# Infini-attention beside a spectral filter on one core: an earlier copy of the products with v, an earlier split for the inverse transform, and maxima that start later

## The chip, the cores and the metric

The kernel runs on one core of one Trainium2 chip. The metric is the device time of one execution in microseconds (us). Three timed runs of the kernel before took 765.5, 766.13 and 767.05 us; the median is 766.13 us. The profile was taken in an execution of its own, which took 768.89 us, of which the recorded span is 767.1 us.

A core has TensorE (PE, matmuls; PEld is its weight load), VectorE (DVE), ScalarE (ACT), GpSimd (POOL) and SyncE (SP). Each works through its own instructions in order. Transfers are issued from the queues of SP and POOL and carried out by 16 DMA engines.

## What is computed

Two independent halves, side by side in the output (2048 rows, 576 columns each):

```python
q,k,v = x@wq, x@wk, x@wv          # 32 heads of width 18, 4 segments of 512 rows
for s in range(4):                # one segment after the other
    p = softmax(q_s k_s^T * scale + mask)       # causal, 512x512 for each head
    a_dot = p @ v_s
    a_mem = phi(q_s) M / (phi(q_s) z + 1e-6)    # memory of the earlier segments
    o_s = g*a_mem + (1-g)*a_dot                 # g = sigmoid(beta), one for a head
    M, z = M + phi(k_s)^T v_s, z + sum(phi(k_s))
a = o @ wo
b = irfft2(rfft2(x) * (w_r + i*w_i))            # 2048 x 576
```

## The kernel before

**Stages.** Four stages follow each other on the core. The forward transform runs first (up to about 103 us of the span). Then come the projections (`projections`, to about 284 us): four segments, in each nine units for q and k (`qk_unit`) and four for v (`v_unit`). Between their matmuls a pace (`Pace`) hands out the vector steps of the transform's middle, among them the last butterflies (`last`, four groups b of ten DVE steps, lines L206 and those around it); `tot` says how many of its steps are spread over the projections, all but 8 of those left. Then the inverse transform (`inverse`, 284 to 373 us) runs together with the first part of the attention (`prologue`), and last the attention loop (`attention`) with its tail.

**Inverse transform.** A loop over u, 16 tiles and two steps to drain. For a tile, `i2` multiplies the split values Y with the table `civ` of that tile (18 matmuls, L296), ACT and DVE evict it as a high and a low part T (L326, L328, L333, L334), and two steps later `i3` multiplies T with `itab` (two halves of 7 matmuls, L307), which is evicted (L312, L314, L315) and stored (`yb`, SP, L316). The split of a tile, `ysplit(u)`, is two ACT copies (high part, L280) and two POOL subtractions (low part, L281); the tiles 0 and 1 are split after the projections, tile u+2 in step u. A table is 384 KB, loaded from POOL's queue (`load_civ`, L266) into one of 3 buffers: three ahead, then u+3 at the end of i2 of tile u.

**Prologue.** In between, the maxima of the scores of the first ten steps are computed (`s1`, three pieces per step: matmuls L624 and L633, reductions on DVE). They need the stacks Qs and Ks, which are gathered on SP's queue in six transfers each (`stack_dmas`, L608, 18 rows of 8 KB, 144 KB each). `inverse` yields 64 times, counted by i from 0; past i=5, three yields of each four go to the prologue (`if i>5 and i%4!=3`). With each piece of `s1` a queue of transfers is worked off, two in each three pieces. Four small transfers write the value -1 into two rows of each Ks buffer (L558, POOL's queue).

**Attention loop.** t counts 133 steps; k=t//4 is a block of four heads, n a group of two blocks. In step t: `s1(t+10)` (maxima for a block that comes later), `s2(t)` (scores once more, exponentials on ACT, L668, L673, L677; after the fourth head of a block four selections of the causal triangle, on POOL for k<29, L680, on DVE after, L681), `pv` for the block before (L696, PSUM tile `pvt`, one buffer), and 1.2 steps of a background queue. `pv` of block k is finished in a step with t%4==3; `pv_out` (L702, ACT) copies it to U in the step after that, and `u_dmas` stores U. A new block's pv begins in the next step with t%4==1 and needs the PSUM buffer back. The background queue holds, for each segment, the memory term (`mem1`, L765 to L772), the combination with it (`combine`: L794, L799, then on POOL the sum `am`, L800, and the low part `ol`, L790, with the high part `oh` on ACT, L789) and the output projection (`oproj`, L815). The stacks of group n+2 and n+3 are queued at the first step of group n.

**Tail.** After the loop the last segment's U goes to memory and returns as `ux` in another layout; `last_tile` scales and combines it (L825, L826), `last_proj` multiplies it with wo (L844).

Of the kernel before, what the change touches and what calls it, by code (L numbers as in the profile page):

```python
# [5 lines left out]
F32=mybir.dt.float32; F32R=mybir.dt.float32r  # L6
# [96 lines left out]
class FFT:  # L103
# [152 lines left out]
    def inv_setup(s,cp):  # L256
        nc,io=s.nc,s.io
        s.cp=cp; s.civ={}
        s.itab=cp.tile([128,2,2,2,FP],F32R,name="itab",bufs=1); s.itab2=cp.tile([128,2,FP],F32R,name="itab2",bufs=1)
        nc.gpsimd.dma_start(s.itab,io["itab"].rearrange("p (h r c f) -> p h r c f",h=2,r=2,c=2))  # L260
        nc.gpsimd.dma_start(s.itab2,io["itab2"].rearrange("p (r f) -> p r f",r=2))
        for u in range(3): s.load_civ(u)
    def load_civ(s,u):
        b,a=divmod(u,4)
        cc=s.cp.tile([128,2,384],F32R,name="civ",bufs=3)
        s.nc.gpsimd.dma_start(cc,s.io["civ"][4*a+b].rearrange("p (h m) -> p h m",h=2))  # L266
        s.civ[u]=cc
    def last(s):

        for b in range(4):  # L270
            x=[s.Z[:,b,c] for c in range(4)]
            yield from s.bf(x,x,True)
            s.done=b
    def ysplit(s,u):
        nc=s.nc; b,a=divmod(u,4); x=s.Z[:,b,a]
        while s.done<b and s.pace.one(): pass
        Y=[s.yp.tile([128,2,356],F32R,name=f"Y{i}",bufs=3) for i in range(2)]
        def parts(y): return y[:,:,:256],y[:,:,256:355].rearrange("p q (k c) -> p q k c",k=3)
        X=x[:,:,:256],x[:,:,None,256:289].to_broadcast([128,2,3,33])
        for z,y in zip(X,parts(Y[0])): nc.scalar.copy(y,z)  # L280
        for z,h,l in zip(X,parts(Y[0]),parts(Y[1])): nc.gpsimd.tensor_tensor(l,z,h.bitcast(F32),op=OP.subtract)  # L281
        s.Yt[u]=Y
    def inverse(s,yl,pp):

# [1 line left out]
        T={}; po={}; Yt=s.Yt  # L286
        def i2(u,cs):
            Y=Yt[u]; cc=s.civ[u]
            p=pp.tile([128,len(cs),256],F32,name="i2",tag="i2")
            for k,c in enumerate(cs):  # L290
                n=0
                for (i,hl) in ((0,0),(0,1),(1,0)):
                    for q in range(2):
                        o=128 if q==0 else 0
                        m=128 if c<2 else 99
                        nc.tensor.matmul(p[:m,k],Y[i][:,q,c*128:c*128+m],cc[:,hl,o:o+256],start=n==0,stop=n==5)  # L296
                        n+=1
            return p
# [21 lines left out]
        for u in range(18):  # L320
            if u>15: flush()
            if u<16:
                h=yl.tile([128,3,256],F32R,name="T0",bufs=3); l=yl.tile([128,2,256],F32R,name="T1",bufs=3)
                T[u]=(h,l)
                p=i2(u,(0,1))
                nc.scalar.copy(h[:,:2],p)  # L326
                if u+2<16: s.ysplit(u+2)
                v.tensor_tensor(l,p,h[:,:2].bitcast(F32),op=OP.subtract)  # L328
                yield
                flush()  # L330
                p=i2(u,(2,))
                Yt.pop(u); s.civ.pop(u)
                nc.scalar.copy(h[:99,2],p[:99,0])  # L333
                v.tensor_tensor(h[64:97,2],p[64:97,0],h[64:97,2].bitcast(F32),op=OP.subtract)  # L334
                if u+3<16: s.load_civ(u+3)
                yield
            if u>1:
                yield from i3(u-2)
                out(u-2)
                s.pace.take(1)  # L340
# [36 lines left out]
class ATT:  # L377
# [147 lines left out]
    def projections(s,xp,tp,pp,wv,pace,hook):  # L525
# [4 lines left out]
        def advance():  # L530
            for l in list(live):
                try: next(l)
                except StopIteration: live.remove(l)
        tot=pace.left-8
        for g in range(4):
            if g<3: xq=[s.xprep(g+1,t,(xp,s.x0)[g%2],xp,[128,512],"xst",2) for t in range(5)]
            for i in range(13):
# [16 lines left out]
    def att_setup(s,cp):  # L554
        nc,io=s.nc,s.io
        s.Qs=[cp.tile([128,8,512],BF,name=f"Qs{i}") for i in range(3)]
        s.Ks=[cp.tile([128,8,512],BF,name=f"Ks{i}") for i in range(4)]
        for i in range(4): nc.gpsimd.dma_start(s.Ks[i][108:110].rearrange("p h c -> p (h c)"),io["neg1"])  # L558
        s.mask=cp.tile([128,512],F32,name="mask"); nc.sync.dma_start(s.mask,io["mask"]); s.tri=cp.tile([128,128],BF,name="tri"); s.idb=cp.tile([128,128],BF,name="idb")
        s.bt,s.gt,s.g1=[cp.tile([128,1],F32,name=n) for n in ("bt","gt","g1")]  # L560
        nc.sync.dma_start(s.bt,io["beta"])
        d=lambda n,sh,dt: s.dp.tile(sh,dt,name=n)
        s.uD=[d(f"uD{i}",[576,512],F32) for i in range(4)]
        s.rD=[d(f"rD{i}",[32,512],F32) for i in range(4)]
        nc.sync.dma_start(s.rD[3][24:32],io["neg1"][0:1].rearrange("o (h c) -> (o h) c",c=512))
        s.dD=[None]+[d(f"dD{i}",[32,512],F32) for i in range(1,4)]
        s.rrD=[d(f"rrD{i}",[96,512],BF) for i in range(4)]
        s.rdD=[None]+[d(f"rdD{i}",[96,512],BF) for i in range(1,4)]
# [210 lines left out]
    def combine(s,g):  # L779

        nc=s.nc; tp=s.tp; xs=s.ux
        s.oh=[None]*5; s.ol=[None]*5
        yield
        yield
        for t in range(7):
            if t>1:
                u=t-2; r=126 if u<4 else 72; x=s.am[u]
                s.oh[u]=tp.tile([126,512],F32R,name="oh",bufs=5); s.ol[u]=tp.tile([126,512],F32R,name="ol",bufs=5)
                nc.scalar.copy(s.oh[u][:r],x[:r])  # L789
                nc.gpsimd.tensor_tensor(s.ol[u][:r],x[:r],s.oh[u][:r].bitcast(F32),op=OP.subtract)  # L790
            if t<5:
                r=126 if t<4 else 72; x=xs[t]
                pb=s.ps.tile([126,512],F32,name="pb",tag="post")
# [3 lines left out]
                    nc.vector.tensor_tensor(s.am[t][:r],x[:r],pb[:r],op=OP.mult)  # L797
                else:
                    nc.vector.tensor_tensor(x[:r],x[:r],pb[:r],op=OP.mult)  # L799
                    nc.gpsimd.tensor_tensor(s.am[t][:r],x[:r],s.am[t][:r],op=OP.add)  # L800
                if t<2: s.later(1,lambda t=t: s.ux_load(g,t+3))
            yield
    def oproj(s,g):
# [53 lines left out]
    def prologue(s):  # L857

        nc,io=s.nc,s.io
        for f in s.stack_dmas(0,0)+s.stack_dmas(0,1): f()  # L860
        yield
        s.load_v(0)
        q=s.stack_dmas(1,0)+s.stack_dmas(1,1)+s.stack_dmas(2,1)+[lambda: s.load_v(1)]
        for i in range(2): yield
        s.masks()
        i=0
        for t in range(10):
            for _ in s.s1(t):
                if q and i%3<2: q.pop(0)()
                i+=1  # L870
                yield
            if t in (3,7): m=s.mpath(t//4); next(m)
            if t in (4,8): next(m); next(m,None)
        assert not q
# [3 lines left out]
    def attention(s,tp,ps):  # L878
# [20 lines left out]
        for t in range(133):  # L899
# [1 line left out]
            if t==3: nc.gpsimd.memset(s.cap,3.0e38)  # L901
            if t==4: nc.gpsimd.affine_select(out=s.cap,in_=s.cap,pattern=[[1,128]],compare_op=OP.is_ge,fill=0.0,base=0,channel_multiplier=-1)
            if hh==0 and qd==0:
                if n+2<16: q+=s.stack_dmas(n+2,0)
                if n+3<16: q+=s.stack_dmas(n+3,1)
                if n+2<16: q.append(lambda n=n: s.load_v(n+2))
            st=t%32
            if 16<=t<21: s.pq_load(1,t-16)
# [26 lines left out]
            steps(b,1)  # L935
            if hh==3 and m is not None: steps(m,1)
            if hh==1 and k+2<32: m=s.mpath(k+2); next(m)
            if t>=8 and t%4==0:
                s.pv_out((t-8)//4)
                if t%8==4:  # L940
                    u=s.u_dmas((t-12)//8)
                    if t<124: s.later(1,lambda u=u: qu.extend(u))
                    else: qu+=u
            for l in list(lane):
# [72 lines left out]
def emit(nc,tc,io):  # L1017
    def pool(es,name,bufs=1,**kw):
        return es.enter_context(tc.tile_pool(name=name,bufs=bufs,reuse_waits="tile",**kw))
    with ExitStack() as L0:  # L1020
# [9 lines left out]
        with tc.manual_schedule():  # L1030
# [5 lines left out]
            with ExitStack() as es:  # L1036
# [3 lines left out]
                def hook(g,i):  # L1040
                    if g==3 and i==9:
# [2 lines left out]
                        F.yp=pool(Ri,"yp",2); F.Yt={}; ci=pool(Ri,"ci")  # L1044
                        tc.swap_default_side()
                        F.inv_setup(ci)
                A.projections(xp,tp,pp,wv,F.pace,hook)
                F.ysplit(0); F.ysplit(1)
            Rv.close(); L1x.close()
            with ExitStack() as L1:  # L1050
                cp2=pool(L1,"cp2"); sm=pool(L1,"sm",2); sp=pool(L1,"sp",3)
# [2 lines left out]
                with ExitStack() as es:  # L1054
# [3 lines left out]
                    A.psm,A.mtag=pi,"mt"  # L1058
                    pr=A.prologue(); next(pr)
                    for i,_ in enumerate(F.inverse(yl,pi)):  # L1060
                        if i>5 and i%4!=3: next(pr,None)
                    for _ in pr: pass
                Ri.close(); Rz.close()
                with ExitStack() as es:
# [20 lines left out]
```

## Time and profile before

| | |
|---|---|
| median of three timed runs | 766.13 us |
| the profiled execution | 768.89 us |
| its span | 767.1 us |
| PE busy | 709.8 us, 93% |
| DVE busy | 549.3 us, 72% |
| ACT busy | 461.5 us, 60% |
| POOL busy | 214.6 us, 28% |
| DMA | 121.06 MB, mean 158 GB/s |

Matmuls overlap in PE's pipeline, and a busy PE is not always one at its peak: the clock that was granted to it stands beside (PEclk, 1.00 is full speed). A row of the timeline has start, duration, engine, line, operation, output and inputs, shapes, and in square brackets the idle time before it with what ended it. A row of the chain has start, duration and what the end of the program hung on. A row of the waits has: engine, line, whom it waited for, then us in total, times, and the longest. A row of the windows has the stretch, its length, the busy time of PE, PEld, DVE, ACT and POOL with the count of instructions, then PEclk, the share of the DMA engines, and GB/s.

### The profile page before, as it was taken

The numbers are of one execution on the slowest core, as the hardware profiler recorded it, in microseconds if no ns is written. First come the engines' busy times: TensorE is split into PE (matmuls) and PEld (weight loads), VectorE is DVE, ScalarE is ACT, GpSimd is POOL, SyncE is SP. The second block draws the span as 40 slices with busy tenths as digits, with TensorE's granted clock in tenths as the row PEclk, the third lists the DMA queues.
The fourth block names the chain that finished last, engine by engine and source line by source line (L and its number), as shares of the span: only waits on it lengthen the run. The fifth ranks groups of instructions, "written<-read, shape, count | busy, mean of one in ns | idle before, by whom it ended". The sixth has DMA issues, their size and how long they took to land.

```text
span 767.1 us, 14531 instructions
## 1 busy us (share of the span) xinstructions
PE 709.8 (93%) x5007; PEld 506.5 (66%) x5007; DVE 549.3 (72%) x1278; ACT 461.5 (60%) x1012; POOL 214.6 (28%) x411
## 2 busy tenths in 40 slices
PE   5998999999999996999988999989999899997897
PEld 5987779789798786999644444434665346652387
DVE  6999878997888883686777778776557575664333
ACT  3666794774783733344577777775556565666421
POOL 2110000101101035355254334452235723347010
PEclk9999999999999997899999999999999899998999
DMA  9874535553642388676477656766355564331141
GB/s 334 284 242 122 165 131 182 199 168 120 210 175 97 146 274 189 157 205 181 132 173 175 173 139 157 178 169 148 100 152 147 138 154 118 99 93 39 26 156 65
DMA packets 83245, 121.06 MB, mean 158 GB/s; under 512 B 11352, under 2 KB 50630, under 8 KB 83036
## 3 DMA queue, kind: packets, MB, share of 16 engines
q1 hardware_dynamic: 76580, 104.11, 47.4%
q0 software_dynamic: 6592, 16.03, 7.4%
q8 instruction: 39, 0.64, 0.4%
q14 instruction: 34, 0.28, 0.1%
HBM read 81.78 MB, written 38.24 MB: 156 GB/s over the span
## 4 chain that ended last, share of the span: by engine, by line
PE 64%; DMA 11%; ACT 4%; DVE 3%; issue 2%; POOL 2%; SPq 1%; ACTq 0%; DVEq 0%; POOLq 0%
PE pj L451 11%; PE pv L696 8%; PE pjv L451 7%; PE s L624 7%; PE po L815 6%; DMA Ks<-qkD 5%; PE i L307 4%; PE i L296 3%; DMA ux<-uD 2%; PE s L667 2%; PE pn L765 2%; PE po L844 2%; PE s L671 2%; PE pm L508 2%; DMA Qs<-qkD 1%
## 5 line engine op out<-in xcount | busy, mean ns | idle before, releaser
L628 DVE CUSTOM_DVE_ANT_0 junk<-s,mask 128x512 bf16<-128x512 f32 (+1 forms) x256 | 141.1, 551 | 67.1 <-PE s L624 63.6
L624 PE MATMUL s<-Ks,Qs 108*128 108x384 bf16 (+3 forms) x512 | 139.7, 304 | 10.2 <-DMA Ks<-qkD 3.0
L634 DVE TENSOR_REDUCE mx<-s 128x4 f32<-128x512 f32 x128 | 87.9, 687 | 19.8 <-PE s L633 18.0
L696 PE MATMUL pv<-P,vs 128*32 128x512 f32 (+3 forms) x1024 | 91.6, 452 | 10.3 <-ACT U L702 9.1
L680 POOL TENSOR_SCALAR_AFFINE_SELECT P<-P 128x512 f32<-128x512 f32 x116 | 70.1, 634 | 74.6 <-ACT P L668 65.1
L624 PEld LDWEIGHTS <-Qs 108*128 108x128 bf16 x512 | 50.8, 99 | 60.3 <-issue 42.4
L668 ACT ACTIVATE P<-s 128x512 f32<-128x512 f32 x128 | 77.3, 604 | 21.8 <-PE s L667 18.2
L677 ACT ACTIVATE P<-s 128x256 f32<-128x256 f32 x128 | 49.4, 386 | 54.6 <-PE s L676 54.3
L673 ACT ACTIVATE P<-s 128x512 f32<-128x512 f32 x128 | 77.0, 602 | 0.7 <-PE s L672 0.5
L451 PE MATMUL pj<-xh,wqkl 128*128 128x512 f32 x180 | 71.1, 395 | 0.0
L451 PE MATMUL pj<-xh,wqkh 128*128 128x512 f32 x180 | 71.0, 395 | 0.0
L451 PE MATMUL pj<-xl,wqkh 128*128 128x512 f32 x144 | 61.8, 429 | 0.0
L667 PE MATMUL s<-Qs,Ks 110*128 110x512 bf16 x128 | 49.1, 384 | 1.9 <-DMA Qs<-mts 1.3
L206 DVE TENSOR_TENSOR Z<-t,t 128x290 f32<-128x290 f32 (+1 forms) x96 | 48.6, 553 | 0.1
L296 PE MATMUL i<-civ,Y 128*128 128x256 f32 (+1 forms) x288 | 43.2, 305 | 5.5 <-DMA civ<-civ 3.0
L451 PE MATMUL pjv<-wvh,xh 128*128 128x288 f32 x160 | 48.1, 303 | 0.0
L451 PE MATMUL pjv<-wvl,xh 128*128 128x288 f32 x160 | 46.2, 295 | 0.0
L206 DVE TENSOR_TENSOR t<-Z 128x580 f32<-128x580 f32 x64 | 45.6, 754 | 0.0
L696 PEld LDWEIGHTS pv<-P,vs 128*32 128x32 f32 x1024 | 23.0, 109 | 32.8 <-issue 21.4
L296 PEld LDWEIGHTS i<-civ,Y 128*128 128x128 f32 (+1 forms) x288 | 39.8, 199 | 7.2 <-issue 3.2
L498 POOL MEMSET vt<- 128x32 f32 x16 | 2.3, 161 | 150.7 <-PE pm L508 129.0
L633 PE MATMUL s<-tri,idb 128*128 128x128 bf16 x256 | 43.4, 221 | 0.0
(166 smaller groups left out, 1652.9 us busy)
## 6 DMA issues: line engine op xcount, KB each, us to landing
qkD<-sp SPq DMA_DIRECT2D x36, 384.0 KB
Qs<-qkD SPq DMA_DIRECT2D x96, 144.0 KB
Ks<-qkD SPq DMA_DIRECT2D x96, 144.0 KB
xin<-xb SPq DMA_DIRECT2D x16, 384.0 KB
cfw<-cfw POOLq DMA_DIRECT2D x16, 384.0 KB, 4.3
civ<-civ POOLq DMA_DIRECT2D x16, 384.0 KB, 5.0
vs<-vD SPq DMA_DIRECT2D x16, 330.0 KB
vD<-vt SPq DMA_DIRECT2D x16, 311.0 KB
```

The lines of the kernel that those rows point to most:

```text
L206: v.tensor_tensor(o,a,b,op=op)
L296: nc.tensor.matmul(p[:m,k],Y[i][:,q,c*128:c*128+m],cc[:,hl,o:o+256],start=n==0,stop=n==5)
L451: s.nc.tensor.matmul(out,a,b,start=i==0,stop=i==len(L)-1)
L624: nc.tensor.matmul(out,Q[:108,h,128*i:128*i+128],K[:108,h,:128*(i+1)],start=True,stop=True)
L628: nc.vector.tensor_tensor_reduce(out=junk[:,:w],in0=src,in1=s.mask[:,512-w:],scale=1.0,scalar=-3.0e38, op0=OP.add,op1=OP.max,accum_out=s.m ...
L634: nc.vector.tensor_reduce(out=s.mx[k][:,hh],in_=pa.rearrange("p (b c) -> p b c",c=128),axis=mybir.AxisListType.X,op=OP.max)
L667: nc.tensor.matmul(p0,kk(0),q(0),start=True,stop=True)
L668: nc.scalar.activation(P[0][:,hh],p0,AF.Exp,scale=SC)
L673: nc.scalar.activation(P[1][:,hh],p1,AF.Exp,scale=SC)
L677: nc.scalar.activation(P[2][:,hh],p2,AF.Exp,scale=SC)
L680: if k<29: nc.gpsimd.affine_select(out=x,in_=x,pattern=pat+[[1,128]],compare_op=OP.is_ge,fill=0.0,base=0,channel_multiplier=-1)
L696: nc.tensor.matmul(s.pvt[32*hh:32*hh+32,128*j:],vt[:,j,19*h:19*h+32],mv[0][:,hh,mv[1]],start=j==0,stop=j==2,skip_group_check=True)
```

## The change

- Split of tiles 0 and 1: issued in the last two v units of the last segment, with the low part on DVE in place of POOL. Tiles 2 to 15 as before.
- `civ`: four buffers, four tables loaded ahead, then table u+4.
- `i2` of tile 1 uses the two PSUM buffers of `i3`.
- The pace leaves 10 steps of the butterflies for the inverse, in place of 8.
- The prologue gets yields past i=11 of `inverse` in place of i=5. Its queue of transfers holds two more stacks (Qs of group 2, Ks of group 3) and is worked off one entry a piece, with one more at pieces 0 and 24. The loop does not load these two stacks any more. The transfers of -1 are issued after the steps 2 to 5 of the prologue.
- `pv_out` and `u_dmas` one step earlier: in the step in which pv is finished.
- `combine`: `am` and `ol` on DVE from step 118 on (`s.now` is the step before).

```diff
-        for u in range(3): s.load_civ(u)
+        for u in range(4): s.load_civ(u)
...
-    def ysplit(s,u):
-        nc=s.nc; b,a=divmod(u,4); x=s.Z[:,b,a]
+    def ysplit(s,u,eng=None):
+        nc=s.nc; eng=eng or nc.gpsimd; b,a=divmod(u,4); x=s.Z[:,b,a]
...
-        for z,h,l in zip(X,parts(Y[0]),parts(Y[1])): nc.gpsimd.tensor_tensor(l,z,h.bitcast(F32),op=OP.subtract)
+        for z,h,l in zip(X,parts(Y[0]),parts(Y[1])): eng.tensor_tensor(l,z,h.bitcast(F32),op=OP.subtract)
...
-            p=pp.tile([128,len(cs),256],F32,name="i2",tag="i2")
+            p=pp.tile([128,len(cs),256],F32,name="i2",tag="i3" if u==1 else "i2")
...
-                if u+3<16: s.load_civ(u+3)
+                if u+4<16: s.load_civ(u+4)
...
-        tot=pace.left-8
+        tot=pace.left-10
...
-        for i in range(4): nc.gpsimd.dma_start(s.Ks[i][108:110].rearrange("p h c -> p (h c)"),io["neg1"])
...
+        eng=lambda: nc.vector if s.now>=117 else nc.gpsimd
...
-                nc.gpsimd.tensor_tensor(s.ol[u][:r],x[:r],s.oh[u][:r].bitcast(F32),op=OP.subtract)
+                eng().tensor_tensor(s.ol[u][:r],x[:r],s.oh[u][:r].bitcast(F32),op=OP.subtract)
...
-                    nc.gpsimd.tensor_tensor(s.am[t][:r],x[:r],s.am[t][:r],op=OP.add)
+                    eng().tensor_tensor(s.am[t][:r],x[:r],s.am[t][:r],op=OP.add)
...
-        q=s.stack_dmas(1,0)+s.stack_dmas(1,1)+s.stack_dmas(2,1)+[lambda: s.load_v(1)]
+        q=s.stack_dmas(1,0)+s.stack_dmas(1,1)+s.stack_dmas(2,0)+s.stack_dmas(2,1)+[lambda: s.load_v(1)]+s.stack_dmas(3,1)
...
-                if q and i%3<2: q.pop(0)()
+                for _ in range(1+(i%24==0)):
+                    if q: q.pop(0)()
...
+            if 2<=t<6: nc.gpsimd.dma_start(s.Ks[t-2][108:110].rearrange("p h c -> p (h c)"),io["neg1"])
...
-                if n+2<16: q+=s.stack_dmas(n+2,0)
-                if n+3<16: q+=s.stack_dmas(n+3,1)
+                if 0<n<14: q+=s.stack_dmas(n+2,0)
+                if 0<n<13: q+=s.stack_dmas(n+3,1)
...
-            if t>=8 and t%4==0:
-                s.pv_out((t-8)//4)
-                if t%8==4:
-                    u=s.u_dmas((t-12)//8)
+            if t>=7 and t%4==3:
+                s.pv_out((t-7)//4)
+                if t%8==3:
+                    u=s.u_dmas((t-11)//8)
...
+                    if g==3 and i>10: F.ysplit(i-11,nc.vector)
                 A.projections(xp,tp,pp,wv,F.pace,hook)
-                F.ysplit(0); F.ysplit(1)
...
-                        if i>5 and i%4!=3: next(pr,None)
+                        if i>11 and i%4!=3: next(pr,None)
```

More of the change, by code (lines that the diff above doesn't have):

```diff
@@ L261, in inv_setup @@
         nc.gpsimd.dma_start(s.itab2,io["itab2"].rearrange("p (r f) -> p r f",r=2))
-        for u in range(3): s.load_civ(u)
+        for u in range(4): s.load_civ(u)
     def load_civ(s,u):
         b,a=divmod(u,4)
-        cc=s.cp.tile([128,2,384],F32R,name="civ",bufs=3)
+        cc=s.cp.tile([128,2,384],F32R,name="civ",bufs=4)
         s.nc.gpsimd.dma_start(cc,s.io["civ"][4*a+b].rearrange("p (h m) -> p h m",h=2))
```

## The prediction

> **What bounds the kernel now.** I read the page first, then the chain of waits, then PE's waits, and then windows and timelines of the places where PE stands idle.
>
> ```profile
> PE 709.8 (93%) x5007; PEld 506.5 (66%) x5007; DVE 549.3 (72%) x1278; ACT 461.5 (60%) x1012; POOL 214.6 (28%) x411
> 274.26 9.30 PE pjv L451 x70
> 291.80 13.62 DMA Ks<-qkD
> 305.42 2.00 issue
> 322.33 1.42 PE i L296 x12
> 327.10 1.42 PE i L296 x12
> 360.43 2.15 PE i L296 x18
> 362.58 1.88 PE i L307 x14
> 372.70 0.34 PE L624 MATMUL s<-Ks,Qs 108*128 108x384 bf16 x1
> ```
>
> PE is busy for 93% of the span, so time can come only from its idle places and from a reduced clock. In the chain the projections' last matmuls end at 274.26+9.30=283.56, the inverse stage ends at 372.70, where the loop's first matmul starts, and between them the chain is not PE's work but a transfer of Ks until 305.42 and 2.00 us more. What would the stage cost with PE never waiting? A tile is 2.15 (i2) plus 1.88 (i3), 4.03 us; tiles that carry three pieces of maxima follow each other at 327.10−322.33=4.77 us, so three pieces cost 0.74. Sixteen tiles and thirty pieces are 16×4.03+10×0.74=71.9 us. The stage takes 372.70−283.56=89.1. Some 17.2 us of it are idle time and half clock, nearly all before 314 us:
>
> ```profile
> 284.56 1.01 PE L296 MATMUL i<-civ,Y 128*128 128x256 f32 x4 [1.01 <-ACT Y L280]
> 286.22 7.49 PE L296 MATMUL i<-civ,Y 128*128 128x256 f32 x32 [0.65 <-POOL Y L281]
> 294.42 2.42 PE L296 MATMUL i<-civ,Y 128*128 128x256 f32 x18 [0.70 <-DVE T L328]
> 301.69 3.04 PE L296 MATMUL i<-civ,Y 128*128 128x256 f32 x18 [2.98 <-DMA civ<-civ]
> 307.43 0.48 PE L624 MATMUL s<-Ks,Qs 108*128 108x384 bf16 x1 [2.70 <-issue]
> 284.00:289.00 5.00, 3.71 (x15) 3.02 (x16) 1.08 (x3) 1.98 (x5) 3.86 (x5) 0.70 0.63 169
> ```
>
> PE waits for the split of tile 0, for its low part, for an eviction before tile 2, for the fourth table, and for Ks; and between 284 and 289 its clock averages 0.70. The attention loop has its own places:
>
> ```profile
> PE pv L696 <- ACT U L702: 9.1, 17, 3.4
> PE s L624 <- DMA Ks<-qkD: 3.0, 3, 1.8
> 384.00:388.00 4.00, 2.25 (x19) 0.87 (x18) 1.88 (x8) 1.81 (x6) 0.76 (x3) 1.00 0.82 192
> 692.32 1.27 POOL L800 TENSOR_TENSOR am<-ux,am 126x512 f32<-126x512 f32 x1
> 692.64 0.63 ACT L789 CAST oh<-am 126x512 fp32r<-126x512 f32 x1
> 695.21 3.62 POOL L800 TENSOR_TENSOR am<-ux,am 126x512 f32<-126x512 f32 x1
> 695.22 2.49 DVE L681 TENSOR_TENSOR P<-P,cap 128x512 f32<-128x512 f32 x4
> 698.86 0.62 ACT L789 CAST oh<-am 126x512 fp32r<-126x512 f32 x1 [2.44 <-POOL am L800]
> 700.28 1.94 PE L696 MATMUL pv<-P,vs 128*32 128x512 f32 x8 [3.43 <-ACT U L702]
> 700.00:705.00 5.00, 4.71 (x14) 1.31 (x14) 0.00 (x0) 2.51 (x6) 4.31 (x5) 0.50 0.02 2
> 711.86 1.06 PE L696 MATMUL pv<-P,vs 128*32 128x512 f32 x8 [0.38 <-ACT U L702]
> 722.07 1.14 PE L696 MATMUL pv<-P,vs 128*32 128x512 f32 x8 [1.21 <-ACT U L702]
> ```
>
> One sum on POOL takes 3.62 us beside DVE's minima, where another took 1.27; ACT stands behind it for 2.44, and with it the copy of U and PE for 3.43; then PE runs at half clock for 5 us.
>
> **The change part by part.**
>
> *Start of the inverse.* With tiles 0 and 1 split during the last v units, PE goes from 283.56 straight into tile 0. The two splits leave the place behind the projections:
>
> ```profile
> 283.88 1.92 ACT L280 CAST Y<-Z 128x512 fp32r<-128x512 f32 x4
> 284.98 3.62 POOL L281 TENSOR_TENSOR Y<-Z,Y 128x512 fp32r<-128x512 f32 x4 [2.47 <-ACT Y L280]
> L328 DVE TENSOR_TENSOR T<-i,T 128x512 fp32r<-128x512 f32 x16 | 11.1, 691 | 21.1 <-ACT T L326 21.1
> 270.00:280.00 10.00, 10.00 (x76) 9.88 (x76) 10.00 (x19) 3.08 (x7) 1.30 (x6) 1.00 1.03 349
> 288.50 6.37 SPq L608 DMA_DIRECT2D Ks<-qkD  x6
> ```
>
> ACT's 1.92 us move to where ACT is busy for 3.08 of 10, and cost nothing. DVE is full there; a subtraction of 512 columns takes 0.69 (L328), with the short one I estimate 1.1 us a tile, 2.2 in all, less two steps that the pace gives up. DVE then ends a microsecond later, in time for the first T, which is needed two tiles on; if it were not, the price is that microsecond. The third and fourth PSUM buffer move the wait for an eviction (0.70) back by one tile. The fourth table, loaded ahead, removes the 2.98.
>
> But all this only brings PE sooner to the next thing that is late, and that is Ks. Its transfers are issued by SP behind the last vt store, at 288.50 as before, and landed at 305.42; PE's first maximum ran at 307.43. I assume the same for the changed kernel. The first piece then stands behind i2 of tiles 0 to 4, i3 of 0 and 1 and half of i3 of tile 2, where it stood behind i2 of 0 to 3 and i3 of 0. PE waits all the same, but has done one i2 and one and a half i3 more: 2.15+1.5×1.88=**5.0 us**. Bounds: if tables 4 to 6, now asked for some 4 us sooner, push Ks back by the time of one 384 KB table at 194 GB/s (2.0 us; between the 169 of 284 to 289 and the 219 of 320 to 330, quoted below), 3.0; if Ks comes before PE does, up to the 17.2. I stay by the lower one, since nothing in the change issues Ks sooner.
>
> *Later in the inverse.* A tile moves one table (384 KB), one output (290) and three stacks (432) in place of two: 1106 KB in 4.77 us, 232 GB/s.
>
> ```profile
> 320.00:330.00 10.00, 10.00 (x82) 9.44 (x80) 8.95 (x22) 4.68 (x13) 4.57 (x6) 1.00 0.76 219
> L608 SPq DMA_DIRECT2D Ks<-qkD x6: 265/305/1914, 288.5 to 293.0; - x6
> 299.75 0.37 SPq L316 DMA_DIRECT2D yb<-yout  x1
> ```
>
> 219 GB/s took 0.76 of the DMA engines, so 232 fit at about 0.8: no cost. Past i=11 the prologue gets 39 of the yields and needs 32, so its pieces still end beside tile 14. The four transfers of -1 leave POOL's queue at the start (cover: POOL waits there anyway) and come back between the tables: nothing.
>
> *Start of the loop.* Twelve stack transfers less in the first steps. The gap around 386 (2.25 us busy of 4) is the 1.8 us wait for Ks, and half of the other 1.2 goes with it: **2.4 us**; bounds 0 and 3.0.
>
> *The copy of U.* One step sooner it stands in ACT's queue behind the exponential of a matmul that PE runs after pv, so ACT can't wait in it, and PE's next pv finds its buffer free. 9.1 us of waits: 5.0 of them are the three late ones above (3.43, 0.38, 1.21), the other 4.1 in 14 places. I take half of these, since DVE and ACT are close behind PE: **2.0** (0 to 4.1). Of the 0.38 and 1.21 I take **1.2** (0 to 1.6).
>
> *Combination on DVE.* From step 118 sum and low part take 0.69 on DVE. The 3.62 us sum goes. What is late next: DVE has six such instructions (two low parts, two products, two sums, 4.1 us) before its minima. They can begin when the high part of 692.64 is there, at 693.3, so the minima start by my estimate at 697.4 rather than 695.22; the first is done at 698.1, and pv can start at 698.2 in place of 700.28: 2.1. The idle time falls from 3.43 to about 1.3, and if the clock stays up, half of the 4.71 us at 0.50 returns: 2.4. Together **4.5** (2.1 to 5.8).
>
> The Trainium skill, "TensorE: Matmul & The Clock Gate", section "Part 1: The HAM clock gate", says that the clock is halved after an idle window of about 3.4 us. The 3.43 before 700.28 agrees; the stretch from 284 to 289, halved after gaps of 1.01 and 0.65, does not. By the rule 1.3 us of idle time are harmless and the sum stands; by that row they may cost the clock again, and the sum is 2.4 smaller. The row at 384 to 388, with 1.75 idle at 1.00, decides for the first.
>
> *Tail.*
>
> ```profile
> 727.85 0.86 PE L696 MATMUL pv<-P,vs 128*32 128x128 f32 x16
> 731.24 0.59 ACT L702 COPY U<-pv 128x512 f32<-128x512 f32 x1
> 737.86 0.38 PE L824 MATMUL pb<-rr,sel 96*126 96x512 bf16 x1 [1.69 <-DVE ux L825]
> ```
>
> The last pv ends at 728.71 and U is copied at 731.24, 2.5 us later, behind the output projection's copies. One step sooner it starts the chain U, rD, ux that long before, which covers the 1.69 us for which PE waits in it: **1.7** (0 to 1.7). PE's work behind stays.
>
> Sum: 5.0+2.4+2.0+1.2+4.5+1.7=16.8 us. Against the profiled execution's 768.89 that is 752.1; that execution is 2.8 above the median of the runs, and from the median 766.13 it is **749.3 us**.
>
> **The rivals.** *Ks comes in time.* If the Ks transfers, without the fourth table and the -1 rows beside them, land by about 301, PE barely waits, and the stage gives halfway between 5.0 and 17.2, 11: 743.3. For it: the queue moved only 169 GB/s around their start. Against: tables 4 to 6 take the place. Chance 0.22.
>
> *The transfers take it back.* Tables asked for sooner delay Ks and each other. A table took 9.1 us to land at the median in this stretch (below), tile 4 needs its table 2×2.15+2×4.03=12.4 us after the start, and it can be asked for only when tile 0 is through and POOL has split tile 2, by my estimate 5.5 us in: 2.2 us late, and 2.0 for Ks. The stage then gives 0.8; if the waits for U don't pay either (2.0 and 1.2), 749.3+4.2+3.2=756.7. Chance 0.20.
>
> ```profile
> DMA to landing us min/median/max: 5.7/9.1/10.9
> ```
>
> *SP's queue becomes the bound.* One Ks issue took 1.91 us, where the median of the six is 0.31. With three stacks and an output store (0.37) a tile, SP's time passes the tile's 4.77 once a stack issue takes over 1.47 us. At 1.91 a tile takes 6.1, ten tiles 13.3 us more, and the start's 5.0 and the loop's 2.4 are lost too: 749.3+13.3+7.4=770.0, slower. Against: single event, in a stretch where twelve stacks were issued back to back. Chance 0.04. The Trainium skill, "DMA: Bandwidth & Descriptors", section "Why a DMA increments its semaphore by 16 and not by 1", says that a transfer is spread over the largest number of engines up to 16 that divides its outer sizes; for 18 rows that is 9 by my reading, and it speaks against three stacks a tile. No view here shows the engines apart.
>
> *Nothing changes*, because DVE and ACT take over as the bound wherever PE stops waiting: within 0.2% of 766.13. Chance 0.04; the idle gaps above are too long for it.
>
> **How the numbers follow.** The forecast, 749.3, has 0.50. Its own bounds put it between 745 and 754. The range goes from 741, below the first rival, to 758, above the second; outside lie the last two rivals (0.08) and the far end of the first. A measurement of this kernel can tell about 0.2% (1.5 us) from no change: faster 0.92, same 0.04, slower 0.04.
>
> **What would show it.** Right: L296 starts by 283.7 at clock 1.00 with no wait for Y; no wait for a table at tile 3; the first L624 at 305 to 307.5, behind 2.5 times L307 x14; the loop's first L667 near 368; no wait for Ks in the loop's first 20 us; L800 at 0.69 on DVE and no PE gap over 1.5 us around its end; waits of pv for U under 3 us in all; no gap before the first L824. Wrong: a first L624 later than 309, waits for `civ` above 3 us, PE at half clock after the combination, or SP's stack issues above 1.5 us.

## The result, and the profile after

The kernel after took 747.5 us, median of six runs (746.4 to 749.99), where the kernel before took 765.85 in the six runs beside it (762.87 to 767.05): a ratio of 0.9771, 95% interval 0.9747 to 0.9795. The profiled execution took 747.36 us, of which the span is 745.5; PE's mean clock over the span rose from 0.976 to 0.988. The forecast was 749.3 us, in a range of 741 to 758. Ratios in this document leave out two executions that stand apart as slow, one of the kernel before (773.58 us) and one of e10_sooner (1692.82 us, its other five 751.43 to 759.45).

The page of the kernel after, two lines of it (its lines of code from the attention on stand one lower than before: L623 was L624, L695 was L696, L701 was L702):

```profile
PE 700.2 (94%) x5007; PEld 502.8 (67%) x5007; DVE 553.9 (74%) x1288; ACT 458.7 (62%) x1012; POOL 203.1 (27%) x401
L695 PE MATMUL pv<-P,vs 128*32 128x512 f32 (+3 forms) x1024 | 89.5, 444 | 0.1
```

The second line is the group of all pv matmuls; behind its last bar stands PE's idle time before them, now 0.1 us. The waits for U are gone. PE's own work is the same 5007 matmuls: of the 21.6 us that the span lost, 9.6 are busy time, with the clock higher, and 12.0 are idle time.

The start of the inverse, PE's timeline of the kernel after, and below it the chain of waits there:

```profile
283.88 5.12 PE L296 MATMUL i<-civ,Y 128*128 128x256 f32 x41
289.23 1.82 PE L296 MATMUL i<-civ,Y 128*128 128x256 f32 x13 [0.23 <-POOL Y L281]
298.94 1.11 PE L307 MATMUL i<-itab,T 128*128 128x290 f32 x7
310.08 0.48 PE L623 MATMUL s<-Ks,Qs 108*128 108x384 bf16 x1 [10.03 <-DMA Ks<-qkD]
```
```profile
289.08 7.22 DMA Qs<-qkD
296.32 13.46 DMA Ks<-qkD
309.78 0.30 issue
```

PE goes from the projections straight into the inverse, and no table is late (no bracket before 310.08 names `civ`). But then it stands still for 10.03 us until Ks is there, at 309.78, where it was there at 305.42 before. The first maximum itself came only 2.65 later than before (307.43 to 310.08), because the 2.00 us that the chain before lists as "issue" between the landing and the matmul are now 0.30; what they were is not known. Windows of the kernel after (stretch, length, busy time of PE, PEld, DVE, ACT, POOL, then PE's clock):

```profile
304.00:309.00 5.00, 0.00 (x0) 0.00 (x0) 0.00 (x0) 0.00 (x0) 0.00 (x0) 0.51 0.86 222
310.00:314.00 4.00, 3.92 (x19) 3.79 (x20) 1.91 (x4) 0.00 (x0) 0.00 (x0) 0.50 0.60 172
384.00:388.00 4.00, 4.00 (x40) 2.13 (x38) 3.21 (x11) 3.27 (x9) 3.86 (x6) 1.00 0.39 111
680.00:685.00 5.00, 3.20 (x30) 1.23 (x26) 4.93 (x8) 4.31 (x12) 1.64 (x4) 1.00 0.15 54
```

In the first, all five engines stand idle and the transfers still run; in the second PE pays once more, at half clock. The third is where the loop waited for Ks: PE is now busy throughout. The fourth is the combination: 1.80 us idle, clock up, and DVE busy for 4.93 of 5.

### The profile page after: what moved, and what is told of

Its sections match the earlier page's. It is cut to its first block, busy times and chain, and to the rows that moved or that the text cites. A ratio compares the mean times of both kernels' runs of the same rounds, so it can differ in the third digit from the quotient of the medians.

```text
span 745.5 us, 14497 instructions
## 1 busy us (share of the span) xinstructions
PE 700.2 (94%) x5007; PEld 502.8 (67%) x5007; DVE 553.9 (74%) x1288; ACT 458.7 (62%) x1012; POOL 203.1 (27%) x401
## 4 chain that ended last, share of the span: by engine, by line
PE 75%; DMA 10%; DVE 7%; ACT 4%; issue 2%; POOL 1%; SPq 1%; ACTq 0%; DVEq 0%; POOLq 0%
PE pj L451 14%; PE pv L695 9%; PE s L623 8%; PE pjv L451 8%; PE po L815 6%; PE i L296 4%; PE i L307 4%; DMA ux<-uD 3%; PE s L666 3%; DMA Qs<-qkD 3%; PE s L670 2%; PE f L142 2%; PE po L844 2%; PE pn L764 2%; PE c L162 2%
## 5 line engine op out<-in xcount | busy, mean ns | idle before, releaser
L623 PE MATMUL s<-Ks,Qs 108*128 108x384 bf16 (+3 forms) x512 | 139.5, 304 | 12.8 <-DMA Ks<-qkD 10.0
L623 PEld LDWEIGHTS <-Qs 108*128 108x128 bf16 x512 | 50.9, 99 | 64.3 <-issue 48.9
L695 PE MATMUL pv<-P,vs 128*32 128x512 f32 (+3 forms) x1024 | 89.5, 444 | 0.1
L667 ACT ACTIVATE P<-s 128x512 f32<-128x512 f32 x128 | 76.2, 596 | 14.7 <-PE s L666 11.8
L672 ACT ACTIVATE P<-s 128x512 f32<-128x512 f32 x128 | 75.8, 592 | 0.5 <-PE s L671 0.5
L632 PE MATMUL s<-tri,idb 128*128 128x128 bf16 x256 | 43.6, 221 | 0.0
L670 PE MATMUL s<-Qs,Ks 110*128 110x384 bf16 x128 | 42.1, 329 | 0.2
L142 PE MATMUL f<-ftab,eh 128*128 128x290 f32 (+1 forms) x160 | 31.9, 319 | 9.8 <-DMA ftab<-ftab 9.8
L296 PE MATMUL i<-civ,Y 128*128 128x256 f32 (+1 forms) x288 | 40.0, 292 | 0.2 <-POOL Y L281 0.2
```

Source lines behind the costliest of these rows:

```text
L623: nc.tensor.matmul(out,Q[:108,h,128*i:128*i+128],K[:108,h,:128*(i+1)],start=True,stop=True)
L667: nc.scalar.activation(P[0][:,hh],p0,AF.Exp,scale=SC)
L670: nc.tensor.matmul(p1[:,:384],kk(1),q(128),start=True,stop=True)
L672: nc.scalar.activation(P[1][:,hh],p1,AF.Exp,scale=SC)
L695: nc.tensor.matmul(s.pvt[32*hh:32*hh+32,128*j:],vt[:,j,19*h:19*h+32],mv[0][:,hh,mv[1]],start=j==0,stop=j==2,skip_group_check=True)
```

## The experiments

**Theory and rival.** The theory is the prediction's: at the start, what decides is when Ks has landed and how much inverse work PE has done by then; the copy of U, the two stacks and the combination each give a small known sum in the loop. The rivals: the time comes from somewhere else in the start (the split and the tables themselves), the parts cost each other something, or the order of the transfers, which the prediction priced at nothing, decides.

Each kernel was timed in five rounds beside the kernel before. Beside its ratio stand stage times from the starts of matmuls in its profiled execution: A, from the inverse's first matmul to the first maximum (the first `s<-Ks,Qs`); B, from there to the loop's first `s<-Qs,Ks` (373.05 before, 0.35 behind the loop's first matmul); C, to the first pv of block 3 (blocks are counted from 0); D, to that of block 28; E, to that of block 31; F, to the end of the span.

| kernel | ratio to before, 95% | A | B | C | D | E | F |
|---|---|---|---|---|---|---|---|
| before | 1 | 22.9 | 65.6 | 39.7 | 276.9 | 32.4 | 45.1 |
| after | 0.9771, 0.9747–0.9795 | 26.2 | 59.9 | 35.8 | 270.3 | 26.6 | 42.7 |
| e1_u_copy | 0.9889, 0.9856–0.9921 | 23.0 | 64.5 | 39.2 | 270.9 | 28.2 | 43.3 |
| e2_combine | 0.9952, 0.9928–0.9976 | 23.2 | 64.5 | 40.2 | 275.2 | 29.5 | 44.7 |
| e3_start | 1.0025, 0.9998–1.0052 | 28.9 | 59.7 | 39.5 | 276.6 | 31.4 | 46.6 |
| e4_later | 0.9700, 0.9666–0.9735 | 26.6 | 53.8 | 35.4 | 271.8 | 28.0 | 42.8 |
| e5_neg_back | 0.9818, 0.9778–0.9858 | 30.0 | 60.2 | 35.6 | 270.7 | 26.6 | 42.9 |
| e6_stacks_back | 0.9858, 0.9820–0.9895 | 26.9 | 60.4 | 39.3 | 271.0 | 26.6 | 43.0 |
| e7_ahead | 0.9746, 0.9702–0.9789 | 23.8 | 61.0 | 36.2 | 267.4 | 26.6 | 44.1 |
| e8_ahead_later | 0.9679, 0.9640–0.9719 | 27.0 | 50.6 | 35.1 | 269.9 | 26.6 | 44.0 |
| e9_neg_only | 0.9975, 0.9947–1.0004 | 21.2 | 65.8 | 39.1 | 274.3 | 32.5 | 43.7 |
| e10_sooner | 0.9825, 0.9784–0.9867 | 25.5 | 64.9 | 36.1 | 269.6 | 26.9 | 43.6 |
| e11_start_neg | 0.9979, 0.9949–1.0009 | 26.3 | 59.4 | 38.6 | 277.2 | 32.8 | 45.5 |
| e12_u_back | 0.9867, 0.9830–0.9903 | 26.7 | 59.8 | 36.5 | 274.4 | 29.7 | 45.9 |

One per cent is 7.7 us. The stages are of single executions; kernels that are alike in a stage differ there by up to 1.1 us in A, 1.6 in B and C, 1.4 in E, 2.9 in F and 4.4 in D.

**The copy of U alone** (before, with this edit):

```diff
-            if t>=8 and t%4==0:
-                s.pv_out((t-8)//4)
-                if t%8==4:
-                    u=s.u_dmas((t-12)//8)
+            if t>=7 and t%4==3:
+                s.pv_out((t-7)//4)
+                if t%8==3:
+                    u=s.u_dmas((t-11)//8)
```

> The kernel before with only the copy of U and its stores one step sooner. If PE waits for that copy in nearly every block and nothing stands close behind (theory U), the distance of one block's pv to the next in the loop falls from 8.51 us to about 8.25, so 31 blocks give 8 us, and with the late waits and the tail's 1.7 some 10 to 12 us: ratio 0.985 to 0.987. If the loop's gain came from the twelve stack transfers that left it (the rival), this kernel gives only the prediction's 2.0+1.2+1.7=4.9 us: ratio 0.9936.

766.61 beside it, 756.94 with it: 9.7 us less by the medians, 8.5 by the ratio (6.1 to 11.0), where the prediction's three terms for it (2.0, 1.2 and 1.7) sum to 4.9. D falls from 276.9 to 270.9, E from 32.4 to 28.2, F from 45.1 to 43.3. The table shows it in D beyond its scatter: the six kernels that copy U late have 274.3 to 277.2, the eight that copy it early 267.4 to 271.8, and the means are 5.5 apart. The first row of pv of three blocks in the kernel before, in the kernel after, and in e12_u_back (below), from their timelines:

```profile
430.45 1.07 PE L696 MATMUL pv<-P,vs 128*32 128x512 f32 x8 [0.32 <-ACT U L702]
438.96 1.06 PE L696 MATMUL pv<-P,vs 128*32 128x512 f32 x8 [0.31 <-ACT U L702]
447.48 1.07 PE L696 MATMUL pv<-P,vs 128*32 128x512 f32 x8 [0.32 <-ACT U L702]
```
```profile
414.07 1.07 PE L695 MATMUL pv<-P,vs 128*32 128x512 f32 x8
422.31 1.06 PE L695 MATMUL pv<-P,vs 128*32 128x512 f32 x8
430.55 1.06 PE L695 MATMUL pv<-P,vs 128*32 128x512 f32 x8
```
```profile
423.44 1.06 PE L695 MATMUL pv<-P,vs 128*32 128x512 f32 x8 [0.31 <-ACT U L701]
431.96 1.07 PE L695 MATMUL pv<-P,vs 128*32 128x512 f32 x8 [0.32 <-ACT U L701]
440.47 1.07 PE L695 MATMUL pv<-P,vs 128*32 128x512 f32 x8 [0.32 <-ACT U L701]
```

The first row shown belongs to block 5 in the kernel before and in e12, to block 4 in the kernel after. A block takes 8.51 us where pv waits 0.32, and 8.24 where it doesn't: 0.27 of the 0.32 comes back, not half.

**The combination alone** (before, with `eng` in `combine` as in the change).

> The kernel before with only the sums and low parts of the combination on VectorE from step 118 on. If the 3.62 us sum on GpSimd is what holds ScalarE and PE at 695 to 700 us, the wait of 3.43 us goes to about 1.3 and the half clock behind it goes: 4.5 us, ratio 0.994. If VectorE's own queue, with its minima behind six more instructions, is late instead, under 1.5 us: ratio 0.998 or more.

763.19 beside 766.61: 3.4 us less; E falls by 2.9, and alone it doesn't keep the clock. Two rows of PE's timeline and a window in this kernel:

```profile
694.74 0.38 PE L667 MATMUL s<-Qs,Ks 110*128 110x512 bf16 x1 [0.36 <-ACT P L668]
696.47 1.57 PE L696 MATMUL pv<-P,vs 128*32 128x512 f32 x8 [0.87 <-ACT U L702]
```
```profile
695.00:700.00 5.00, 4.03 (x14) 1.05 (x13) 4.10 (x7) 2.90 (x7) 0.11 (x1) 0.69 0.03 7
```

With U late as well, pv waits 0.87, and the clock falls to 0.69 in these 5 us, which it does not in the kernel after. And e1 shows the other side: with the copy of U early and the sum left on POOL, E also falls, by 4.3. Four rows of e1's timeline:

```profile
688.35 5.77 DVE L681 TENSOR_TENSOR P<-P,cap 128x512 f32<-128x512 f32 x4
688.51 1.72 POOL L800 TENSOR_TENSOR am<-ux,am 126x512 f32<-126x512 f32 x1
690.18 1.72 POOL L790 TENSOR_TENSOR ol<-am,oh 126x512 fp32r<-126x512 f32 x1
691.87 1.70 POOL L800 TENSOR_TENSOR am<-ux,am 72x512 f32<-72x512 f32 x1
```

The same pair meets as before, but now it is DVE's four minima that stretch, 5.77 us in place of 2.49, beside three POOL instructions of some 1.7 us each, where such a one took 1.27 before. So the two edits share one stall: they take 4.3 and 2.9 off E alone and 5.8 together. The 1.4 between the sums is no more than E's scatter, so it is the rows that show it. The Trainium skill, "SBUF — State Buffer", section "SBUF: two separate sides", says that a port pair shared by DVE and GpSimd is an exclusive lock, so that whichever instruction starts second stands still. The rows agree that one of the two stands still: in the kernel before it was POOL, whose sum (3.62) ended 1.12 us after the last minimum, here it is mostly DVE, by 3.28. They don't show who gives way: before, the sum started at 695.21 and the minima at 695.22, and it was the sum that waited. Moving the work to DVE ends it: the minima of the kernel after take 2.49.

**The start alone, and with the -1 rows moved.** e3_start is before with the early split on DVE, four tables, the PSUM buffers, the pace and `i>11`, which were not timed apart; e11_start_neg has the -1 transfers moved as well; e9_neg_only is before with only these moved; e5_neg_back is after with them back at their old place:

```diff
+        for i in range(4): nc.gpsimd.dma_start(s.Ks[i][108:110].rearrange("p h c -> p (h c)"),io["neg1"])
...
-            if 2<=t<6: nc.gpsimd.dma_start(s.Ks[t-2][108:110].rearrange("p h c -> p (h c)"),io["neg1"])
```

> The kernel before with only the inverse's start changed: tiles 0 and 1 split in the projections, four tables, the two PSUM buffers, the pace, and the prologue past i=11; stacks, the -1 rows, U and the combination as before. If Ks is the bound of this stage, PE stands idle for some 8 to 10 us before the first maximum, the stage is 3 to 5 us shorter than before, and the time falls by as much: ratio 0.9935 to 0.996. If the shorter wait were for work that this part removes (the rival), the first maximum comes without a long wait and the stage is 8 us shorter or more: ratio 0.9895 or less.

> The changed kernel with the four transfers of -1 back where they were, on GpSimd's queue at the start of the inverse. If they hold up the Qs and Ks transfers (theory: they are what made the start alone lose time), SP takes some 5 us rather than 2.44 to issue the six Qs transfers, the first maximum runs at about 314 us in place of 310.1, and the time is about 4 us above the changed kernel's 747.5: ratio to the kernel before 0.979 to 0.982. If they are free, as the prediction had it, the first maximum stays within 1 us of 310 and the ratio at 0.975 to 0.977.

> The kernel before with only the four transfers of -1 moved behind the steps 2 to 5 of the prologue. If they hold up Qs and Ks by themselves, as putting them back into the changed kernel suggests (4.2 us), the first maximum, at 307.4 us before, comes 2 to 4 us sooner and the time falls by as much, as far as the late fourth table does not hold PE instead: ratio 0.995 to 0.998. If they only hurt beside tables that are asked for sooner, nothing changes: ratio 0.998 to 1.002.

> The kernel before with the start of the inverse as in the start-alone run and also the four transfers of -1 moved behind the steps 2 to 5. The start alone was 2.4 us above the kernel before; if the -1 transfers were its only fault, this is 1.8 to 3.5 us below it: ratio 0.995 to 0.998, with the first maximum at about 310 us. If the start needs the other parts too, it stays at or above the kernel before: ratio 1.000 or more.

The start alone gains nothing (769.04 beside 766.61, ratio 1.0025, interval with 1 in it): B falls by 5.9, as the count of work says, and A rises by 6.0, because the first maximum comes at 314.29. With the -1 transfers moved, A rises by only 3.5 (765.12 beside 767.19; 1 is just in the interval). Back in their old place in the changed kernel they cost 0.0047 of the time, 3.6 us, with an interval that just reaches 0, and 3.8 of A; from e3 to e11 it is 0.0046, with an interval of 0.0040 to either side. In the kernel before, moving them alone gives 1.7 in A and no clear difference in the total. SP's issues and the first maximum in the kernel after, then in e5:

```profile
287.76 2.44 SPq L607 DMA_DIRECT2D Qs<-qkD  x6
290.25 6.35 SPq L607 DMA_DIRECT2D Ks<-qkD  x6
```
```profile
288.22 4.93 SPq L608 DMA_DIRECT2D Qs<-qkD  x6
293.45 8.23 SPq L608 DMA_DIRECT2D Ks<-qkD  x6
314.03 0.48 PE L624 MATMUL s<-Ks,Qs 108*128 108x384 bf16 x1 [11.55 <-DMA Qs<-qkD]
```
```profile
285.24 2.01 POOL L558 DMA_DIRECT2D Ks<-neg  x4 [0.39 <-issue]
```

Qs's issues begin 0.46 us later, Ks's end at 301.68 where they ended at 296.60. So four small transfers on POOL's queue, whose issue takes 2.01 us (last row, e5), go with slower issues on SP's queue and a later landing of the stacks. Their time matters: in the kernel before POOL issued them from 288.54, behind the split, when all six of Qs were out, and Qs's issues took 2.44; with the split off POOL they come from 285.24 (e5) and 286.62 (e3), ahead of Qs, and those issues take 4.93 and 5.30. So the early split also moved them ahead of Qs. Why a few rows slow the issues was not settled.

**The work ahead of the first maximum.** e10_sooner and e4_later are after with `i>5` and `i>19` in place of `i>11`.

> The changed kernel with the prologue past i=5 again. The prediction counted the gain of the start by what stands ahead of the first maximum in PE's queue while Ks is on its way: past i=5 that is one i2 and one and a half i3 less, 5.0 us. By this the wait for Ks grows from 10.0 to 15 us and the time by 5.0: ratio 0.981 to 0.984. If fewer tables on the way let Ks land sooner (the rival), the first maximum comes at 307 us or before and the time grows by 2 us or less: ratio 0.975 to 0.979.

> The changed kernel with the prologue past i=19 in place of i=11, so that two more tiles of the inverse stand ahead of the first maximum in PE's queue. If the 10.0 us wait is for Ks alone and the tables are in time, two tiles (2x4.03=8.1 us) run in it, the wait falls to about 2 us, and the time falls by 8 us or, with the clock kept up, 10: ratio to the kernel before 0.964 to 0.967, that is 738 to 740 us. If the DMA engines as a whole are the bound until 310 us (share above 1.1 in that stretch), the added tiles wait for their tables instead, and the time stays within 2 us of 747.5: ratio 0.975 to 0.979.

B is 64.9, 59.9 and 53.8 us with 5, 11 and 19: the later the first maximum stands in the order, the less is left behind it, whatever A does. The total follows: e10 is 0.0054 above after (4.1 us, of 5.0 counted), e4 0.0071 below (5.4 us), less than the 8 expected. The rows of e4's timeline that say why:

```profile
299.34 2.37 PE L296 MATMUL i<-civ,Y 128*128 128x256 f32 x18 [1.20 <-DMA civ<-civ]
311.62 0.32 PE L623 MATMUL s<-Ks,Qs 108*128 108x384 bf16 x1 [0.89 <-DMA vs<-vD]
313.84 1.21 PE L307 MATMUL i<-itab,T 128*128 128x290 f32 x7 [1.72 <-DVE yout L315]
```

The wait before the first maximum is down to 0.89 (the profile names the load of vs, which no maximum reads), so it has little left to give; a table is 1.20 late, and an eviction by DVE 1.72.

**The stacks in the loop again** (after, with the prologue's queue and the loop's loads as before).

> The changed kernel with the two stacks of groups 2 and 3 loaded by the loop again, as before. If the loop's early waits for Ks are worth what the comparison of the loops shows beyond the copy of U, the first blocks of the loop take 3 to 4 us longer (second pv at 21 us from the loop's start in place of 18.1) and the ratio is 0.979 to 0.981. If the prediction's 2.4 holds, the ratio is 0.978 to 0.979. If the inverse gains from carrying two transfers a tile in place of three, up to 2 us of this comes back before the loop: the loop starts sooner than 85.6 us after the projections' end.

0.0087 above after: 6.7 us, with an interval of about 3.5 to either side and more than either expectation; in the stages C is 3.5 longer, A, B and D together 1.9, which is within their scatter. Over all kernels C is 38.6 to 40.2 with the stacks loaded in the loop and 35.1 to 36.5 without. The gap at 386 is back, and this time the clock falls with it. A row of PE's timeline, and the window that the kernel after has at 1.00:

```profile
384.11 0.48 PE L623 MATMUL s<-Ks,Qs 108*128 108x384 bf16 x1 [2.04 <-DMA Ks<-qkD]
```
```profile
384.00:388.00 4.00, 3.89 (x21) 1.49 (x22) 1.53 (x4) 1.78 (x4) 0.54 (x1) 0.57 0.90 183
```

**Qs and Ks first in SP's queue** (e7_ahead: after, with the loads of the mask, of beta and of a row of -1 issued behind the first twelve stack transfers; e8_ahead_later: the same with `i>19`).

```diff
...
         for f in s.stack_dmas(0,0)+s.stack_dmas(0,1): f()
+        nc.sync.dma_start(s.mask,io["mask"])
+        nc.sync.dma_start(s.bt,io["beta"])
+        nc.sync.dma_start(s.rD[3][24:32],io["neg1"][0:1].rearrange("o (h c) -> (o h) c",c=512))
```

> The changed kernel with the first Qs and Ks transfers put ahead of mask, beta and the row of -1 for rD in SP's queue, nothing else. If the wait before the first maximum is set by when SP issues Ks, the transfers start some 2.5 us sooner and the first maximum runs at about 307.5 in place of 310.1: 2 to 2.5 us less, ratio 0.972 to 0.974. If the DMA engines are full until then and set the landing, it moves by less than 1 us: ratio 0.975 to 0.978.

> The changed kernel with both the order of SP's queue of the run before and the prologue past i=19. With the first maximum past i=19 alone PE still stood idle before it, and the time was 743.0. If both effects add, 740 to 741 us: ratio 0.966 to 0.968. If PE is then no longer late for Ks but for tables or evictions, 742 to 744: ratio 0.969 to 0.972.

In e7 the first maximum comes at 307.78, 2.3 sooner than after, about as much as the first issue of Qs (285.68, 2.1 sooner). Now a table is late, and what the profile names at the maximum is beta, which no maximum reads:

```profile
299.77 3.89 PE L296 MATMUL i<-civ,Y 128*128 128x256 f32 x18 [2.70 <-DMA civ<-civ]
307.78 0.48 PE L621 MATMUL s<-Ks,Qs 108*128 108x384 bf16 x1 [3.18 <-DMA bt<-beta]
```

746.45 us; its ratio cannot be told from that of after. e8 takes 742.29 us, ratio 0.9679 (0.9640 to 0.9719): with e4 it is the best version found. Both beat the kernel before and the kernel after; the two can't be told apart. Their B is the shortest of the table.

**The copy of U late again** (after, with the copy of U and its stores at their old place).

> The changed kernel with the copy of U and its stores back where they were. If the copy's gain does not depend on the other parts, this loses the 9.7 us that the copy alone won: ratio 0.987 to 0.991, and a block of the loop takes 8.5 us again in place of 8.25. If part of that gain is the same idle time that the combination and the stacks remove, 6 to 8 us: ratio 0.983 to 0.987.

0.0096 above after: 7.4 us, with an interval of about 3.4 to either side. In the profiled execution, which stands 1.65 above its median, D is 4.1 longer, E 3.1, F 3.2, C 0.7. With e1 this settles from both sides that the term is well above the 4.9; whether the other edits share a part of e1's gain is within the noise.

## Why the prediction was right or wrong

**The start: right mechanism, landing wrong.** It had PE wait for Ks and the gain as the work placed ahead of that wait, 5.0 us. B fell by 5.7; e10 gives 5.0 of B back, as counted, and e4 takes off 6.1 where two tiles count 8.1. The step that failed is "I assume the same for the changed kernel", with Ks issued "at 288.50 as before": Ks was issued from 290.25, the first maximum came at 310.08, not 307.43, 2.65 later, and the loop's first `s<-Qs,Ks` 3.0 sooner (373.05 to 370.01). That is the lower bound (3.0), though not shown to be for its reason: Qs's issue began 1.74 us later in SP's queue (286.02 to 287.76), and the chain's Qs transfer took 7.22 us in place of 4.84; Ks's own piece, 13.46, is as before (13.62). Of the 1.74, 0.79 is the last store of vt, issued at 284.84 in place of 284.05, and 0.98 the issue of the mask behind it, 1.36 us in place of 0.38. That issue takes 0.38 to 0.46 in all four kernels with three tables ahead and 0.82 to 1.55 in the eight with four in which it stands there; whether the table or the early split does it was not tested. The sign given as wrong, "a first L624 later than 309", came true. The split itself went as costed: DVE's row gives 1.08 for the two subtractions of one tile, a long and a short one, and PE did not wait for Y of tiles 0 and 1.

```profile
282.58 1.08 DVE L281 TENSOR_TENSOR Y<-Z,Y 128x512 fp32r<-128x512 f32 x2
```

**The -1 transfers: wrong.** "Nothing" was the price of moving them. In the changed kernel it is 3.6 us (e5), and without it the start gives no gain at all (e3). With the rows moved, the start alone (e11) is at best a little faster than before. The cover that was named, POOL waiting there anyway, covers POOL's time and not SP's issues.

**Later in the inverse and the queue of SP: right.** Three stacks a tile cost nothing that shows; B lies within 1.6 us in all kernels with `i>11`, with two stacks a tile (e3, e6, e11) or three. The rival of SP's queue did not happen: the longest issue of a stack in the inverse of the kernel after took 1.35 us.

**Start of the loop: under.** 2.4 was taken, with 3.0 as the upper bound; C fell by 3.9, of which e12 gives 0.7 to U, and e6 measures 3.5 in C alone. The bounds took only the gap around 386.

**The copy of U: mechanism right, size wrong.** No pv waits for U in the loop's list of waits any more, and no wait of that size took its place. The step that failed is "I take half of these, since DVE and ACT are close behind PE": 2.0, with 4.1 as the upper bound. Through block 28 it gives 4.8 (e12: 0.7 in C, 4.1 in D), since 0.27 of each 0.32 came back, and most blocks in which no wait is listed became shorter too, by 0.13 to 0.26; the list leaves out waits under 0.15 us, and there are many of 0.1. Of D's 6.6 between the two kernels e12 accounts for 4.1; the rest is no more than D's scatter, and the means of all late and all early kernels are 5.5 apart.

**The end of the loop: right in sum.** 1.2 for U's late waits and 4.5 for the combination make 5.7; E fell by 5.8. How the 5.7 falls to the two was a guess, since they share the stall. The working of the queue of DVE held. DVE's rows of the kernel after:

```profile
679.78 0.98 DVE L790 TENSOR_TENSOR ol<-am,oh 126x512 fp32r<-126x512 f32 x1 [1.09 <-ACT oh L789]
681.40 0.69 DVE L800 TENSOR_TENSOR am<-ux,am 126x512 f32<-126x512 f32 x1
683.93 2.49 DVE L680 TENSOR_TENSOR P<-P,cap 128x512 f32<-128x512 f32 x4
```

The sum takes 0.69, the minima begin 4.15 us after the first low part (4.1 was estimated), and pv starts at 684.66, right behind the first of them. DVE is what is late next, as said. The clock stayed at 1.00, as the sum had it. The row that the prediction rested this on, 1.75 us idle at 1.00 from 384 to 388, was no safe ground: at the same place e6 waits 2.04 us and its clock is 0.57, and in e2, with the combination on DVE, the clock fell.

**The tail: right, a little under.** 1.7 was taken; F fell by 2.3, within its scatter. U is copied right behind pv, and 0.57 of the 1.69 us stays:

```profile
707.72 0.86 PE L695 MATMUL pv<-P,vs 128*32 128x128 f32 x16
708.64 0.59 ACT L701 COPY U<-pv 128x512 f32<-128x512 f32 x1 [0.42 <-PE pv L695]
716.61 0.38 PE L824 MATMUL pb<-rr,sel 96*126 96x512 bf16 x1 [0.57 <-DVE ux L825]
```

In sum: 16.8 us forecast; the medians differ by 18.35, and the two profiled executions by 21.5, of which 2.8 are that execution of before standing above its median. That the total came out this close is partly luck, because errors cancel: 2.0 too much at the start, some 4 too little for U and the stacks together. The start's 3.0 already holds what moving the -1 transfers gives.

## What to carry to other kernels

A wait of 0.3 us that the bound engine met in most iterations came back almost whole here, and blocks that list none gained too: where waits recur like this, multiply by the iterations, and do not take half of the listed waits. Where a stage waits for a transfer, count the work that stands ahead of the wait in the engine's order, and move the first consumer back until the wait is gone. Before a load is asked for earlier or a small one is moved, look at the issue times on the other queues too, since four tiny transfers cost here as much as the start brings.

## What the runs showed of the hardware

- The clock does not follow the length of the gaps. In e2 PE waited 0.36 and 0.87 and ran at 0.69 of the clock from 695 to 700; in e1 it waited 2.15 us at 694.77 (timeline row below) and the clock stayed at 1.00. What the falls have in common is how little PE worked in one stretch of 3.41 us. In each trace the clock is halved for whole multiples of 3.41 us (10.24 from 304.07 in the kernel after, 3.41 from 696.89 in e2; only the one at a program's end is cut short), and within a trace the starts are whole multiples of that step apart, so that they lie on one grid. In e2 PE was busy for 2.04 us in the stretch before the fall; in e1 the wait is cut in two by a border of the grid, and PE was busy for 2.18 and 2.40.

```profile
694.77 0.38 PE L667 MATMUL s<-Qs,Ks 110*128 110x512 bf16 x1 [2.15 <-ACT P L668]
```

The windows on this grid, two of e2, then two of e1:

```profile
693.48:696.89 3.41, 2.04 (x12) 0.74 (x14) 3.38 (x7) 3.21 (x9) 0.61 (x1) 1.00 0.03 6
696.89:700.30 3.41, 3.41 (x12) 0.94 (x5) 2.21 (x4) 1.18 (x4) 0.00 (x0) 0.50 0.02 5
```
```profile
690.44:693.85 3.41, 2.18 (x12) 0.60 (x12) 3.41 (x3) 0.96 (x3) 3.41 (x3) 1.00 0.02 5
693.85:697.27 3.42, 2.40 (x16) 0.79 (x15) 0.66 (x2) 3.42 (x9) 2.78 (x3) 1.00 0.02 3
```

Over the fourteen traces, each of the 45 falls comes after a stretch with PE busy for at most 2.20 of the 3.41 us. None of the more than 2700 stretches with more was followed by one. Between 1.65 and 2.21 both happen (22 falls, 23 without), below 1.65 there was always a fall. This is read off the traces and was not tested by a run made for it.

The rule that the prediction cited from the Trainium skill, "TensorE: Matmul & The Clock Gate", section "Part 1: The HAM clock gate", a halving after an idle window of about 3.4 us, agrees with the 10.03 us before the first maximum and with 680 to 685 in the kernel after, but not with e2, where PE was far from idle. The same section also calls the window free-running, which fits; these are single executions of each kernel, though, so that stays open.

- Issues on one queue took longer while small transfers were under way from another: six issues of Qs took 4.93 us (e5) and 5.30 us (e3) with the four -1 transfers ahead of them, and 2.44 to 2.53 us without in eleven of the other twelve kernels (3.15 us in e10).
